# Linear attention and an FFN on one core: all scores in 64x64 tiles, part of the state sum on TensorE, another order of steps

## The chip, the cores and the metric

One core of a Trainium2 chip runs the whole program. The metric is device time in microseconds, the median of three executions; the time before is 443.19 us (442.01 to 443.64).

## The reference

Inputs r, k, v, w have the shape (4, 8, 768, 48): batch, heads, time, channels. For each batch and head a state of 48x48 runs along time, and its output goes through a token mix of rank 32 and an FFN (384 to 1536 to 384 channels).

```python
for t in range(S):
    cur = np.einsum('bhd,bhe->bhde', u[None] * kt, vt)
    y[:, :, t] = np.einsum('bhd,bhde->bhe', rt, state + cur)
    state = wt[:, :, :, None] * state + np.einsum('bhd,bhe->bhde', kt, vt)
# x: y as (batch, time, 384)
h = x.transpose(0, 2, 1) @ U @ V
u = x + h.transpose(0, 2, 1)
out = u + np.maximum(u @ w_ch1, 0.0) @ w_ch2
```

## The kernel before

Time is cut into chunks of 128; a batch has six, so there are 24, numbered g, with c = g % 6 the place in the batch. The heads lie as four pairs j, the two heads of a pair i on partitions 0 to 47 and 64 to 111. `chunk(g)` (line 349) lists the steps of a chunk, each for one engine:

- LW, LRK, LKR, LV load decays, r and k (channels by time), r and k by rows, and v; all loads are issued from SP's queue.
- F and Q (VectorE, L393 and L408) are products of decays along time. RP (L416) multiplies r by Q, KS (L421) k by F; each has VectorE and POOL to choose from. T copies the chunk's total decays, R inverts them.
- PR (L497, first batch) multiplies r and k, MD sums it by products with u; later chunks use RK, RU and RED. SEL and SEL2 (L465 on ScalarE, L472 on POOL) put the result on the diagonals of A.
- AM (L561, L553) multiplies k and r into scores in PSUM (`aps`). For chunks of which `swaps(g)` is true (line 48: g of 12 and more, and the last of a batch, g = 11 among them) it uses 64x64 tiles, four side by side in TensorE, and skips the quarter above the diagonal. For pairs 2 and 3 the rows of k then lie with swapped halves of time; others use 48x128 products, two side by side. CP (L566, L568) merges the scores under the diagonal into A.
- KT and KN turn k by TensorE and ScalarE, KD on VectorE from g = 12 on. DS (L575) multiplies turned k and v into `dS`, ZA (L604) adds the old state Z on VectorE, ZM (L613 on ScalarE, L615 on VectorE) multiplies by the next chunk's total decay.
- YA (L633, L643) multiplies A and v, YZ (L656, L660) adds the old state's part, XE (L677) copies the output, XT/XN or XD turn it.

`token_mix(b)` has GA, G4, SELM (L787), GS, GSL for a batch, `make_u` HP, UADD, UH (L840, L842) and UL (L846) for one of seven blocks of 384 or 512 columns, `ffn` twelve UP of nine products (L879), HH (L884 ScalarE, L886 VectorE), HL (L890), and twelve DN of nine products (L913). The FFN weights are brought into two parts by `split_raw` (C2, C3, E, ADD, HI, SUB with L341), and checks of weights (CK, CM) run late.

The order of the steps is written out: `ORDER` (line 66) is a text with three digits for each step: two for its number, one with two meanings (`plan`, line 135): odd, and the step runs on its other engine; half of it is `lead`, the count of warming products that `lead()` (line 202) has TensorE do just before the step. Those multiply a block of zeros (`blank`, bf16, 128x384, L200) into the place that the step's own products overwrite, and are no part of the result. Each engine and each queue takes its steps in the order of this text and waits in place. `aps` and `dS` exist once, so a step that writes them waits for the reader before.

Of the kernel before, what the change touches and what calls it, by code (L numbers as in the profile page):

```python
# [42 lines left out]
TURN_K_DVE, TURN_X_DVE = [12, 13, 14, 15, 16, 17, 18, 19, 20, 21, 22, 23], [12, 13, 14, 15, 16, 17, 18, 19, 20, 21, 22, 23]  # L43
W_MAX, W_MAX_BITS, DECAY_MIN = 1.25, 0x3FA00000, 1e-16
HIGH_MIN, HIGH_END = 1.125 * 2.0**-15, 122880.0


def swaps(g):

    return g >= 6 and (g in TURN_K_DVE or g % NCH == NCH - 1)  # L50


def channel_order():
# [18 lines left out]
    "7d04v07e00A07y04905G13l00b03L00p01C04W00c04AE7-04sC0B01D04t04Y00q00e04Z04X10f00d11E07f10g04a05H04f05I03m01F0"
    "5407h04w04z07l04B04+08011G04-04b07m14x08100z05J64y08505K05001H10r15L04c00s00u07g05M08415O05108Q00v00h05N00-0"
    "5P00i07a07n17q05Q08201005R07r00+07o00j08315S08O05T00t01100w01W08Y07u87p07v08R05U05Y01I05c05V00k07s05Z05W05a0"
    "5d08C01P07w05X18E05e00x01X01205b15f15p01K00y18Z17x01d07t11J01L08D01311R05q05s06205t01M08801N01e05u01Q01f02A0"
    "8905r01O08T05j06308a16507+01Y01g06401Z05g08A18B18G06601h08F05k01k01S01a06701r08b08J05h01T05i02B08S18W07c15l0"
    "8q08K08r01b06W06X01U01i05m08c11y08U05-05n01j11s08X01c11V06001t08+08d15y01l01m01u05o05v01v06109G08H05z08L02C0"
    "8V08g01z02301n02D08s08t01o01w05+05w08h05x08I16802E02H01x11p01q16B06E06C01+08l02406902508y01-02608v06D06A08w0"
    "2708m02I02802009P08-12109406F09018u18e06G02O08f02912V06Y08x02F18i09602G19109502216H02c06K02W02P06a02J02X02K0"
    "2d08z09216Z19H02L09J09312Q02M09L02Y02q09i08j06L06I09706b02N06e08n02Z02R08k12e02j02S02T06M02a09B06f09C02U02f0"  # L80
    "9M09K12g09Q06c0980BL09l08o02k08p06N02b16g16d16h19n09N0BB09D08M02l08N06Q09k02s07A02h12r06O06P06x02m07B02i19m0"
    "9I06y06z06J0BC09R17C06R02n02o17D0Bl02p12t02u07E09E09S09j0Bm07F0BM02v09s06S09t09O16r02w09o09q09F06s06l0BE06t0"
    "6m09Y0Bn16n07709T0Bo09U19r0BG0781990790BK06T09V19W0Bb06o06U06u09u19v09p1Bc09Z09X06V09a09y09w06p09d0BH09A09e0"
    "DB06v09b09x09z06q0Be06w0BI1Bg06+07106-06i0BJ0BF07009f07409+09c19-0BV0DC0BN0BR06j0Bj0750720Bh0Bd0BS0DD0C50BO0"
    "CF06k0CE0BD0730A00BP07G09g0C60760C80Br0BT07H0A107I0Bk0Bp1CX07J0A20BQ0C90Bf1BW0CY0BZ0DE0Ca0A30Bi19h0BU0Bq0A40"
# [74 lines left out]
def rwkv_moe_kernel(ctx, tc, wT, rkT, vN, vS, rkN, uB, uT, uD, U, V, w1, w2, out):  # L160
# [1078 lines left out]
```

## Time and profile before

| | |
|---|---|
| median of three runs | 443.19 us |
| the profiled execution | 442.49 us, span 440.8 us |
| TensorE, VectorE, ScalarE, POOL busy | 422.5, 349.9, 184.4, 131.7 us |
| products of the FFN (L879, L913) | 1512 of 3931 on TensorE |
| moved by DMA | 57.27 MB |

The span is what the instructions of one execution cover; the rest of its time lies around it. A TensorE product's duration in the rows overlaps the next one's, so the cost of a group of products is read from its start to the start of what follows.

### The profile page before, as it was taken

Reading aid. Unit: us, or ns where it says so; the run is one execution under the profiler, and the core shown is the slowest. Engines: PE = TensorE matmul, PEld = TensorE weight load, DVE = VectorE, ACT = ScalarE, POOL = GpSimd, SP = SyncE. Lnnn points to the kernel's source line nnn. Section 1 sums busy time; section 2 is a strip of 40 time slices with the busy share of each in tenths; the row PEclk is TensorE's granted clock in tenths of the full one; section 3 lists DMA queues with packets and bytes.
Section 4 is the critical chain, followed back from the end, with each engine's and each line's share of the span. In section 5 each row is a group of like instructions: output and inputs, shape, how many; then the busy total and the mean of one; then the engine's idle time right before and its main releaser. Section 6 shows DMA issues by size and latency. Waiting matters only on the chain.

```text
span 440.8 us, 10001 instructions
## 1 busy us (share of the span) xinstructions
PE 422.5 (96%) x3931; PEld 364.3 (83%) x3931; DVE 349.9 (79%) x796; ACT 184.4 (42%) x517; POOL 131.7 (30%) x157
## 2 busy tenths in 40 slices
PE   7989999999999999999999999999999999999993
PEld 4876788999999898878777788887766889999992
DVE  8899889999899999999999999999886224315610
ACT  5798888884245225363033423131741023301200
POOL 5665456334575375421145211051001001000000
PEclk8578999999999999999999999999999999999998
DMA  8996494556745341635064024245051022212001
GB/s 264 314 315 249 156 325 119 156 171 194 207 156 159 121 137 27 196 82 153 18 208 155 2 73 146 86 145 167 5 175 38 0 97 83 91 54 91 0 24 40
DMA packets 23912, 57.27 MB, mean 130 GB/s; under 512 B 2864, under 2 KB 7856, under 8 KB 23856
## 3 DMA queue, kind: packets, MB, share of 16 engines
q1 hardware_dynamic: 23856, 56.54, 40.3%
q8 instruction: 33, 0.54, 0.5%
q14 instruction: 23, 0.19, 0.1%
HBM read 51.81 MB, written 4.72 MB: 128 GB/s over the span
## 4 chain that ended last, share of the span: by engine, by line
PE 51%; DVE 37%; issue 4%; ACT 3%; DMA 2%; SPq 0%; DVEq 0%; ACTq 0%
PE f L913 19%; PE f L879 19%; DVE kn L696 8%; DVE xn L731 6%; DVE hid L890 4%; DVE Q L408 3%; DVE A L566 3%; DVE F L393 3%; PE aps L561 2%; PE y L633 2%; DVE xn L729 1%; DVE xT L835 1%; ACT A L465 1%; DMA w<-in_wT 1%; PE y L643 1%
## 5 line engine op out<-in xcount | busy, mean ns | idle before, releaser
L879 PE MATMUL f<-u,w1h 128*128 128x384 f32 (+1 forms) x504 | 147.6, 364 | 1.8 <-DVE hid L890 1.8
L913 PE MATMUL f<-hid,w2h 128*128 128x384 f32 (+1 forms) x504 | 149.1, 365 | 0.0
L879 PEld LDWEIGHTS f<-u,w1h 128*128 128x128 f32 x504 | 92.9, 188 | 14.4 <-DVE hid L890 3.2
L913 PEld LDWEIGHTS f<-hid,w2h 128*128 128x128 f32 x504 | 93.0, 188 | 9.9 <-issue 1.1
L884 ACT ACTIVATE hid<-f 128x384 fp32r<-128x384 f32 (+1 forms) x70 | 37.2, 541 | 142.5 <-PE f L879 97.7
L879 PE MATMUL f<-u,w1l 128*128 128x384 f32 (+1 forms) x252 | 90.8, 360 | 0.0
L913 PE MATMUL f<-hid,w2l 128*128 128x384 f32 (+1 forms) x252 | 90.8, 360 | 0.0
L890 DVE SCALAR_TENSOR_TENSOR hid<-f,hid 128x384 fp32r<-128x384 f32 (+1 forms) x84 | 49.8, 606 | 19.4 <-ACT hid L884 18.6
L913 PEld LDWEIGHTS f<-hid,w2l 128*128 128x128 f32 x252 | 47.5, 188 | 4.6
L879 PEld LDWEIGHTS f<-u,w1l 128*128 128x128 f32 x252 | 47.4, 188 | 4.2
L696 DVE STREAM_TRANSPOSE kn<-rk 32x128 f32<-32x128 f32 x160 | 48.3, 302 | 2.4
L465 ACT ACTIVATE A<-ident,dv 128x128 f32<-128x128 f32 x140 | 43.9, 393 | 4.9 <-DVE dv L451 4.8
L324 POOL TENSOR_TENSOR cva_w<-cva_w,raw_w 128x384 int32<-128x384 int32 x24 | 25.4, 1063 | 47.3 <-DVE cva_w L317 21.1
L416 POOL TENSOR_TENSOR rk<-rk,Q 128x512 f32<-128x512 f32 x19 | 23.5, 1236 | 46.9 <-DVE Q L408 33.0
L846 POOL TENSOR_TENSOR u<-xT,u 128x512 fp32r<-128x512 f32 (+1 forms) x11 | 13.4, 1232 | 78.5 <-DVE u L842 68.1
L408 DVE TENSOR_TENSOR_SCAN Q<-w,starts,qd 128x258 f32<-128x258 f32 x48 | 33.2, 733 | 0.2
L393 DVE TENSOR_TENSOR_SCAN F<-w,qd 128x259 f32<-128x259 f32 x48 | 30.4, 675 | 1.8 <-DMA w<-in_wT 1.6
L931 DVE TENSOR_TENSOR xT<-f,xT 128x384 f32<-128x384 f32 (+1 forms) x21 | 12.6, 605 | 23.4 <-PE f L913 23.3
L731 DVE STREAM_TRANSPOSE xn<-xT 32x192 f32<-32x192 f32 x80 | 29.6, 369 | 2.1 <-ACT xT L677 0.9
L421 POOL TENSOR_TENSOR rk<-rk,F 128x512 f32<-128x512 f32 x15 | 17.9, 1196 | 15.5 <-DVE F L393 8.2
L886 DVE TENSOR_SCALAR hid<-f 128x384 fp32r<-128x384 f32 (+1 forms) x14 | 8.2, 584 | 15.9 <-PE f L879 15.9
L472 POOL TENSOR_SCALAR_AFFINE_SELECT A<-dv 128x128 f32<-128x128 f32 (+1 forms) x39 | 11.6, 333 | 30.2 <-PE f L913 20.2
(124 smaller groups left out, 571.4 us busy)
## 6 DMA issues: line engine op xcount, KB each, us to landing
raw_w<-in_w SPq DMA_DIRECT2D x48, 384.0 KB, 3.6
rk<-in_rkT SPq DMA_DIRECT2D x24, 512.0 KB, 4.9
kr<-in_rkN SPq DMA_DIRECT2D x18, 384.0 KB, 4.2
w<-in_wT SPq DMA_DIRECT2D x24, 260.0 KB, 3.4
v<-in_vS SPq DMA_DIRECT2D x24, 224.0 KB, 3.4
out_dram<-xT SPq DMA_DIRECT2D x12, 192.0 KB, 3.2
out_dram<-xT SPq DMA_DIRECT2D x9, 256.0 KB, 2.9
raw_V<-in_V SPq DMA_DIRECT2D x8, 96.0 KB, 3.6
```

Of the source, the lines that this page charges most:

```text
L324: lambda: nc.gpsimd.tensor_tensor(out=d["to"].bitcast(I32), in0=d["a"].bitcast(I32), in1=d["e"], op=ALU.add),
L393: nc.vector.tensor_tensor_scan(out=back(F), data0=back(st["w"]), data1=back(qd, OVER * h), initial=1.0, op0=ALU.mult, op1=ALU.add)
L408: nc.vector.tensor_tensor_scan(out=st["Q"][:, a:e], data0=st["w"][:, a:e], data1=qd[:, a - OVER * h : e - OVER * h], initial=starts[:, h : ...
L416: ENG[eng].tensor_tensor(out=rk[:, 0], in0=rk[:, 0], in1=Qv, op=ALU.mult)
L421: ENG[eng].tensor_tensor(out=rk[:, 1], in0=rk[:, 1], in1=F5, op=ALU.mult)
L465: nc.scalar.activation(to, one, AF.Copy, scale=dv[:, NP * i + j : NP * i + j + 1])
L696: nc.vector.transpose(a, b)
L731: nc.vector.transpose(to[q, :, :, r], src[r, :, :, q])
L879: nc.tensor.matmul(ps, wt[:, f, ct, :], u[ct][:, z], start=(m == 0), stop=(m == 8))
L884: nc.scalar.activation(h[:, 0], d["ps", f], AF.Relu)
L890: nc.vector.scalar_tensor_tensor(out=h[:, 1], in0=d["ps", f], scalar=0.0, in1=h[:, 0].bitcast(F32), op0=ALU.max, op1=ALU.subtract)
L913: nc.tensor.matmul(d["o", ct], wt[:, 4 * ct + part, f - 3 * part, :], hid[f][:, z], start=(part == 0 and m == 0), stop=(part == 3 and m == 8),
```

## The change

Five things change.

1. `scores` uses 64x64 tiles for every chunk: eleven more, g = 0 to 10. Two ScalarE activations at the program's start write zeros into the parts of `aps` that the tiles never write, since the merge now always reads whole halves.
2. The array of k comes from the host with swapped halves of time for pairs 2 and 3. So `scale_k` (KS) and `prod` (PR) are two multiplications, one for pairs 0 and 1, one for pairs 2 and 3 with the other operand's halves read crosswise. `diag` on POOL is always three instructions; none of the chunks g = 0 to 10 ran it on POOL before.
3. For g = 1 to 4 `state_add` (DS) multiplies the identity by the old Z first and adds k and v on top, in PSUM. ZA is gone there, and DS waits for the old state's ZM.
4. `ORDER` is another text. Decoded, it has 1418 steps (four ZA fewer), and eight warming products in place of 29: six before YA 6 and two before UP 0.4; before, they stood ahead of YA 2 (9), XT 0.2 (7), KT 4 (6), YA 5 (3) and YA 6 (4). The first FFN step is number 301 (300 before), with the same TensorE steps in front of it in another order, and the same TensorE steps stand behind SELM 3.
5. By that text some steps change their engine (counts before and after). On VectorE: ZM 4 and 0, KS 9 and 7, UH 8 and 2, HI 3 and 1, SUB 18 and 16, T 7 and 6, DV 0 and 1, HH 14 and 17, RK 5 and 6, RP 5 and 6. What VectorE gives up goes to ScalarE (ZM, UH, HI, T) or POOL (KS, SUB). SEL on POOL: 5 and 8; SEL2: 8 and 6.

Between the last UL of block 0 and GSL 3 VectorE has in the new text one KS, two SUB, three ZM, one CK, one HL, three UH, two HI and one T fewer, and five HH and two UL more.

```diff
+ADD_Z_PE = (1, 2, 3, 4)
...
-def swaps(g):
-
-    return g >= 6 and (g in TURN_K_DVE or g % NCH == NCH - 1)
...
+    for a in range(2):
+        part = aps_all[HP * a : HP * a + HP, :, NQ * (1 - a) : NQ * (2 - a), 0:HP]
+        nc.scalar.activation(part, blank[HP * a : HP * a + HP].rearrange("p (i j t) -> p i j t", i=2, j=NQ), AF.Copy)
...
+        def by_halves(eng, to, k, x):
+
+            a, b = slice(0, NQ), slice(NQ, NP)
+            ENG[eng].tensor_tensor(out=to[:, a], in0=k[:, a], in1=x[:, a], op=ALU.mult)
+            to, k, x = (t[:, b].rearrange("p j (h l) -> p j h l", h=2) for t in (to, k, x))
+            ENG[eng].tensor_tensor(out=to, in0=k, in1=x[:, :, ::-1, :], op=ALU.mult)
...
-            ENG[eng].tensor_tensor(out=rk[:, 1], in0=rk[:, 1], in1=F5, op=ALU.mult)
+            k = st["rk"][:, 1]
+            by_halves(eng, k, k, F5)
...
-                ENG[eng].tensor_tensor(out=st["kr"], in0=st["rk"][:, 0], in1=st["rk"][:, 1], op=ALU.mult)
+                by_halves(eng, st["kr"], st["rk"][:, 1], st["rk"][:, 0])
...
-            for j in range(NP):
-                for i in range(2):
-                    r = slice(64 * i, 64 * i + D)
-                    nc.tensor.matmul(aps[:, i, j, :], rk[r, 1, j, :], rk[r, 0, j, :], start=True, stop=True)
+            for j in range(NQ):
+                for h in range(2):
+                    for i in range(2):
+                        r = slice(64 * i, 64 * i + D)
+                        for a in range(2):
+                            jj, s0 = j + NQ * (a ^ h), HP * h
+                            k0 = HP * a
+                            nc.tensor.matmul(
+                                aps[HP * a : HP * a + HP, i, jj, s0:P], rk[r, 1, jj, k0 : k0 + HP], rk[r, 0, jj, s0:P],
+                                start=True, stop=True,
+                            )
...
+                    to = dS[r, j, i * D : i * D + D]
+                    if z_pe:
+                        nc.tensor.matmul(to, ident[:, r], old["Z"][:, j, i * D : i * D + D], start=True, stop=False)
+                    nc.tensor.matmul(to, kn[:, j, r], v[:, j, r], start=not z_pe, stop=True)
...
-            if c > 0:
+            if not fresh:
                 za = step("ZA " + nm, "DVE", add_z, [ds, old["z"]], take=[buf["Z"]], use=[buf["dS"], old["buf"]["Z"]])
...
+    kT = chunked(k, 0.0)
+    kT[:, :, :, NQ:] = np.roll(kT[:, :, :, NQ:], HP, axis=4)
+    rkT = np.stack([chunked(r, 0.0), kT], axis=3)
```

## Rows read from the trace of the kernel before

**Rows 1.** The page: busy time of each engine; TensorE's clock in 40 slices.

```profile
PE 422.5 (96%) x3931; PEld 364.3 (83%) x3931; DVE 349.9 (79%) x796; ACT 184.4 (42%) x517; POOL 131.7 (30%) x157
...
PEclk8578999999999999999999999999999999999998
```

**Rows 2.** Windows: us, busy time by engine, granted clock, DMA share, GB/s.

```profile
8.00:28.00 20.00, 19.01 (x170) 16.59 (x172) 18.57 (x39) 16.47 (x55) 13.87 (x13) 0.50 0.97 311
28.00:34.80 6.80, 4.68 (x89) 3.83 (x82) 6.74 (x16) 6.80 (x24) 3.31 (x3) 1.00 0.92 313
34.80:38.20 3.40, 3.40 (x39) 1.86 (x36) 3.40 (x7) 3.00 (x11) 2.14 (x3) 0.50 1.02 394
38.20:62.60 24.40, 24.14 (x423) 18.66 (x419) 22.17 (x44) 20.42 (x56) 11.72 (x11) 1.00 0.61 208
62.60:327.60 265.00, 261.27 (x2651) 222.54 (x2649) 253.27 (x592) 117.45 (x322) 93.61 (x114) 1.00 0.43 131
327.60:433.40 105.80, 105.01 (x559) 98.23 (x559) 38.85 (x86) 17.21 (x47) 3.20 (x3) 1.00 0.16 51
```

**Rows 3.** Chain of waits, whole span: start us, us, what.

```profile
40.51 1.09 PE aps L561 x16
...
127.75 0.83 PE aps L553 x32
...
337.35 12.36 PE f L913 x54
```

**Rows 4.** Groups by line and shape, TensorE, 8 to 28 us.

```profile
L561 PE MATMUL aps<-rk 48*128 48x128 f32 x48 | 6.2, 437 | 1.0 <-DVE A L568 0.7 <-POOL rk L416 0.3
...
L575 PE MATMUL dS<-v,kn 128*48 128x48 f32 x32 | 1.8, 285 | 0.0
```

**Rows 5.** Timeline of TensorE, 30 to 63 us: start us, us, what.

```profile
34.04 2.34 PE L200 MATMUL y<-blank 128*128 128x384 bf16 x9 [2.12 <-ACT xT L677]
36.30 1.08 PE L633 MATMUL y<-A,v 128*32 128x128 f32 x16
...
42.24 1.30 PE L200 MATMUL trx<-blank 128*128 128x384 bf16 x7
43.38 0.49 PE L750 MATMUL trx<-ident,xT 128*128 128x128 f32 x3
...
47.97 0.56 PE L575 MATMUL dS<-v,kn 128*48 128x48 f32 x16
48.47 0.65 PE L633 MATMUL y<-A,v 128*32 128x128 f32 x16
...
50.81 0.65 PE L200 MATMUL y<-blank 128*128 128x384 bf16 x3
51.39 0.64 PE L633 MATMUL y<-A,v 128*32 128x128 f32 x16
```

**Rows 6.** Line L421 on VectorE (min/median/max ns), then groups by line and shape.

```profile
L421 DVE TENSOR_TENSOR rk<-rk,F x9: 678/685/932, 19.3 to 298.6; 128x512 f32<-128x512 f32 x9
...
L421 POOL TENSOR_TENSOR rk<-rk,F 128x512 f32<-128x512 f32 x15 | 17.9, 1196 | 15.5 <-DVE F L393 8.2 <-DVE kr L497 3.9 <-DMA rk<-in_rkT 3.4
...
L604 DVE TENSOR_TENSOR Z<-dS,Z 128x384 f32<-128x384 f32 x16 | 8.8, 547 | 0.1
...
L341 DVE TENSOR_TENSOR w2l<-cva_w,w2h 128x384 fp32r<-128x384 f32 x9 | 4.8, 547 | 0.1
...
L613 ACT ACTIVATE Z<-dS,tots 128x96 f32<-128x96 f32 x16 | 4.1, 336 | 0.0
...
L615 DVE TENSOR_TENSOR Z<-Z,tots 128x384 f32<-128x384 f32 x4 | 2.2, 539 | 0.0
...
L842 DVE CAST u<-xT 128x384 fp32r<-128x384 f32 x6 | 2.1, 352 | 0.0
...
L324 POOL TENSOR_TENSOR U_sb<-cva_U,raw_U 128x192 int32<-128x192 int32 x1 | 0.6, 604 | 0.0
```

**Rows 7.** Waits of VectorE, 8 to 62.6 us: us in total, times, longest.

```profile
DVE A L568 <- PE aps L561: 1.8, 3, 0.7
```

More of the change, by code (lines that the diff above doesn't have):

```diff
@@ L72 @@
[L72 to L76, printed above, removed]
@@ L461, in diag @@
                     to, one = A[:, i, j], ident
-                    if swap and j >= NQ:
+                    if j >= NQ:
                         to, one = (x.rearrange("p (a b) -> p a b", b=HP) for x in (to, one))
@@ L466, in diag @@
                 return
[L467 to L490 removed]
+            for js, ts, base in (
+                (slice(0, NQ), slice(0, P), 0), (slice(NQ, NP), slice(0, HP), HP), (slice(NQ, NP), slice(HP, P), 0),
+            ):
+                n = ts.stop - ts.start
+                nc.gpsimd.affine_select(
+                    out=A[:, i, js, ts],
+                    in_=dv[:, NP * i + js.start : NP * i + js.stop].unsqueeze(2).broadcast_to([P, NQ, n]),
+                    pattern=[[0, NQ], [1, n]],
+                    compare_op=ALU.is_equal,
+                    fill=0.0,
+                    base=base,
+                    channel_multiplier=-1,
+                )
         if by_pe:
@@ L545, in scores @@
             lead(aps[:, 0])
[L546 to L568 removed]
+            for j in range(NQ):
[8 more added lines that the diff above has]
+                                start=True, stop=True,
+                            )
+        def merge():
+            to, new = (t.rearrange("p i j t -> p i (j t)") for t in (st["A"], st["aps"]))
+            nc.vector.copy_predicated(to, mask2, new)
         def state_add():
@@ L594, in chunk @@
         if on:
-            ds = step("DS " + nm, "PE", state_add, [kn, lv], take=[buf["dS"]], use=[buf["kn"], buf["v"]])
+            ds = step(
+                "DS " + nm, "PE", state_add, [kn, lv] + ([old["z"]] if z_pe else []), take=[buf["dS"]],
+                use=[buf["kn"], buf["v"]] + ([old["buf"]["Z"]] if z_pe else []),
+            )
             st["ds"] = ds
-            zuse = [buf["dS"]] if c == 0 else [buf["Z"]]
+            fresh = c == 0 or z_pe
+            zuse = [buf["dS"]] if fresh else [buf["Z"]]
             def new_z():
@@ L607, in decay @@
                 nxt = sts[g + 1]["tot"]
-                if c == 0:
+                if fresh:
                     new_z()
-                src = dS if c == 0 else st["Z"]
+                src = dS if fresh else st["Z"]
                 if eng == "ACT":
@@ L617, in decay @@
                     )
-            if c > 0:
+            if not fresh:
                 za = step("ZA " + nm, "DVE", add_z, [ds, old["z"]], take=[buf["Z"]], use=[buf["dS"], old["buf"]["Z"]])
             st["z"] = step(
-                "ZM " + nm, "DVE", decay, [ds] if c == 0 else [za],
-                take=[buf["Z"]] if c == 0 else [], use=zuse, alt="ACT",
+                "ZM " + nm, "DVE", decay, [ds] if fresh else [za],
+                take=[buf["Z"]] if fresh else [], use=zuse, alt="ACT",
             )
@@ L964, in recurrence @@
                 nc.sync.dma_start(chunks(rt), rb[:, 0, j])
-                nc.sync.dma_start(chunks(kt), rb[:, 1, j])
+                for h in range(2):
+                    s0 = HP * (h ^ (j >= NQ))
+                    nc.sync.dma_start(chunks(kt)[:, :, HP * h : HP * h + HP], rb[:, 1, j, :, s0 : s0 + HP])
                 nc.vector.memset(vt, 0.0)
@@ L1189, in ordered @@
         a = a.copy()
-        for g in range(B * NCH):
-            x = a[g // NCH, g % NCH, :, NQ * 2 :]
-            if swaps(g):
-                x[:] = np.roll(x, HP, axis=0)
+        a[:, :, :, NQ * 2 :] = np.roll(a[:, :, :, NQ * 2 :], HP, axis=2)
         return a
```

139 lines of the change are left out of this document (46 added, 93 removed).

## The prediction

> **What bounds the kernel now.** I read the page first: TensorE is busy 96% of the span and VectorE 79%, and the slices show the clock of TensorE below full only in the first tenth [rows 1]. So the windows by stage come next [rows 2]. Between 8 and 28 us TensorE is busy 19.0 of 20.0 us, but at a granted clock of 0.50, that is 1.2 GHz, and the DMA engines are at 0.97. From 28 to 34.8 us the clock is full; in 34.8 to 38.2 it is at 0.50 again; after that it stays at 2.4 GHz. In 38.2 to 62.6 us, up to the first FFN product, TensorE is busy 24.1 of 24.4 us and VectorE 22.2. From 62.6 to 327.6 us, where chunks and FFN blocks alternate, TensorE has 261.3 of 265.0 us and VectorE 253.3. After 327.6, where the last chunk's token mix is summed, TensorE works 105.0 of 105.8 us and VectorE a third of that. Third, the chain of waits: there 54 products of L913 run without a gap, 12.36 us at 337.35 us [rows 3]. This last stage is set by its product count alone. The change leaves that count and the step that opens the stage (SELM 3) as they are, so the end moves by as much as SELM 3 moves. Before it, TensorE and VectorE are both close to full: a saving counts only where both get it. I therefore sum each engine up to the first FFN product and from there to SELM 3, and take the smaller gain.
>
> **Part 1, up to the first FFN product (62.6 us).** Eight chunks' scores (g = 0 to 7) lie here, the same set in both orders.
>
> Scores on TensorE. Sixteen 48x128 products take 1.09 us from start to start at full clock; the 32 tiled ones, which g = 11 and later already use, take 0.83 [rows 3]. Five chunks save 0.26 each, 1.3 us. Three run at half clock, 6.2 us for 48 products, or 2.07 each [rows 4]. No row shows the tiled form at half clock; its bounds are 2.07 (nothing saved) and 1.24 (0.83 saved). By the ratio 0.83 to 1.09 it is 1.58; I take 0.5 saved each, 1.5 us.
>
> State sums. DS takes 0.50 us at full clock (47.97 to 48.47 us) [rows 5]; two at half clock take 1.8 us [rows 4]. DS 1 to 4 double their products: 0.9 for DS 1 and 0.5 for each of the others, 2.4 us more (bounds 1.2, if the identity products overlap well, and 3.6).
>
> Warming products. Ahead of YA 2, XT 0.2, KT 4, YA 5 and YA 6 stand 29 of them: nine from 34.04 to 36.30, seven from 42.24 to 43.38, three from 50.81 to 51.39 [rows 5], and ten more at 1.14 / 7 = 0.163 us, together 2.26 + 1.14 + 0.58 + 1.63 = 5.6 us. The eight of the new order cost 1.3, so 4.3 us go. TensorE alone would gain 1.3 + 1.5 + 4.3 - 2.4 = 4.7 us, by the bounds 2.0 to 6.9.
>
> VectorE. Removed: four ZA at 0.547, one ZM at 0.539 (the decay goes to ScalarE, four activations of 0.336), one KS at 0.685 [rows 6], 3.4 us. Added: one RP (as KS, 0.685) and one RK (0.55, as other operations on 384 columns), a small copy of 0.1 to 0.2, and seven multiplications cut in two: 512 columns take 0.685 and 384 take 0.547, so the fixed part is near 0.13; with some overlap I take 0.1 each, 0.7. Net 3.4 - 2.1 = 1.3 us less. VectorE also waited 1.8 us in three places for scores [rows 7], which come earlier without the warming products. It can gain 3.1 us at most; I take half the waits, 1.3 + 0.9 = 2.2.
>
> POOL. A KS of 512 columns takes 1.196 us and 192 columns 0.604 [rows 6], so the slope is 1.85 ns and the fixed part 0.25 us, which each cut repeats. Off the path POOL has room (11.7 busy of 24.4 us [rows 2]), but the first KS and the RP queued behind it stand before the first scores, with the cut product PR 0 ahead of them: 0.25 + 0.1 = 0.35 us later (bounds 0 and 0.6). I charge 0.2, for TensorE was behind its inputs soon after.
>
> Loads on SP's queue. By the shapes, up to the fifth chunk's decays the old order moves 7.74 MB and the new one 7.52; at 311 GB/s [rows 2] that is 0.7 us earlier. The keys of chunk 1 come behind a weight piece, 1.93 MB instead of 1.55, 1.2 us later. I take zero: these ends cancel, and the half-clock queue of TensorE covers the late one. The two activations that clear parts of aps stand at ScalarE's start, before the first decay lands, and cost nothing; without that cover they would be two operations of at most 0.5 us.
>
> New wait. DS 1 to 4 now wait for the preceding ZM on ScalarE. YA and YZ of the same chunk are queued behind them on TensorE, and ZM of this chunk waits for DS. Before, ZA on VectorE took that wait. The new order puts at least three other TensorE steps between one DS and the next (YA 2, YZ 2 and MD 5 before DS 3), which cover the ZM between them, so I cost it at nothing; a late ZM would show as a gap like the one before 34.04 us, 2.1 us [rows 5].
>
> Part 1 together: 2.2 - 0.2 = **2.0 us less** (bounds: 2.1 + 0.6 - 1.3 = 1.4 more, if that gap comes back and POOL's cut costs its bound; 3.1 less).
>
> **Part 2, 62.6 to 327.6 us.** On TensorE only the scores of g = 8, 9 and 10 shrink, 0.8 us. VectorE loses one KS, two SUB, three ZM, one weight check and one HL, the last four kinds near 0.55 [rows 6], 4.5 us; three UH and two HI of 0.35 [rows 6], 1.8; it gains five HH and two UL of 0.55 to 0.69, 3.9 to 4.8, and three cuts, 0.3. Net 1.2 to 2.1, so 1.7 us less. VectorE has 11.7 us idle here and TensorE 3.7 [rows 2]: both queues are almost full, and a shorter one gives back part of the other's waits. I take 1.7 us, VectorE's sum. The most is TensorE's, 0.8 + 3.7 = 4.5; the least, a new order that makes one more wait like the one at 34.04, is 2.1 worse [rows 5].
>
> On POOL and VectorE together: one of nine VectorE KS took 0.932 us against a median of 0.685 [rows 6], so a neighbour seldom costs anything. The Trainium skill, SBUF — State Buffer, section Who interferes with whom, says that a VectorE instruction with two SBUF inputs and a GpSimd instruction that reads SBUF contend, and the later one fully blocks. By that rule, two KS and two SUB moved to POOL could come back to VectorE as blocked time, 2.5 us: the sum would be 3.7 - 2.5 = 1.2 us less, 442.0. The trace bears it out in one instruction of nine and by 0.25 us, so I keep the row's price.
>
> **The sum.** 2.0 + 1.7 = 3.7 us less. The profiled execution took 442.49 us with a span of 440.8; the median of the three runs is 443.19, 0.7 above. On the median: **439.5 us**. A measurement of this kernel can tell about 0.5%, 2.2 us, from no change.
>
> **Rivals.** *No change to be told, 441.7 us.* The order only trades waits: VectorE stays the later engine up to SELM 3, warming products stood in waits anyway, and the moved work returns as waits for ScalarE and POOL. For it: VectorE's own relief is only 1.3 + 1.7 us, ScalarE gets five more decays and six UH, and at 28 to 34.8 it was busy 6.8 of 6.8 us [rows 2]. Against it: 1.8 us of VectorE's waits were for scores [rows 7]. With half of VectorE's relief left, 1.5 us less.
>
> *Slower, 447.5 us: the clock.* Full clock came at 28 us, was lost after the gap before 34.04, and came back after the nine products; thirteen of the others stand right behind [rows 2, 5]. If the sparse head of the new order leaves TensorE at 1.2 GHz for 16 us more up to 62.6, its work there takes 8 us longer: 439.5 + 8 = 447.5. It decides from about 12 us more at half clock on (6 us, which turns the 3.7 gained into 2.3 lost). For it: 19.0 of 20.0 busy us did not raise the clock in 8 to 28. Against it: KT 2, KT 3, YA 1 and YZ 1 stand together in both orders, and were under way when the clock rose.
> The Trainium skill, TensorE: Matmul & The Clock Gate, Why this matters for your kernels, advises no long idle gaps between bursts, since an idle engine is throttled again. By that rule the missing products would cost just this; the trace agrees in the one dip, which followed the idle 2.1 us.
>
> *Better than the sum, 435.5 us:* the waits of Part 2 shrink to TensorE's own bound: 3.1 + 4.5 = 7.6 us less.
>
> **How the numbers follow.** The forecast has 0.52, no change 0.24, the clock 0.16, the better case 0.08. Faster by over 0.5% is 0.52 + 0.08 = 0.60, same 0.24, slower 0.16. The range holds the forecast, the no-change case and the better one: 435.5 at the low end, and at the high end 445.0, the no-change case with the worst new waits of both parts (441.7 + 1.4 + 2.1 = 445.2). The clock case is mostly left out.
>
> **What would show it.** Right: scores of 0.83 us from g = 0 on at full clock and near 1.6 at half; no ZA before chunk 7 on VectorE; DS 1 to 4 near 1.0 us; the first L879 near 60.6 us; SELM 3 near 324; the same 105.8 us behind it. Wrong: a granted clock of 0.50 after 38 us; TensorE idle before DS; SELM 3 not earlier though the first L879 is, which would mean that Part 2 took the gain back.

## The result, and the profile after

The changed kernel takes **435.92 us** (median of four runs, 435.45 to 438.02) against 442.6 for the kernel before beside it: ratio 0.9855 (95% interval 0.9826 to 0.9885), 6.4 us less. The forecast was 439.5, 3.7 less: the sign was right and the size a little over half, with 1.8 us in a place where nothing was forecast. The profiled execution took 435.73 us with a span of 433.9.

The page, busy time and TensorE's clock, beside [rows 1]:

```profile
PE 417.4 (96%) x4150; PEld 361.9 (83%) x4150; DVE 344.5 (79%) x791; ACT 188.7 (43%) x536; POOL 137.7 (32%) x182
...
PEclk8586999999999999999999999999999999999998
```

Windows of the changed kernel at its own stages, beside [rows 2] (columns as there):

```profile
8.00:24.60 16.60, 15.91 (x209) 14.46 (x210) 16.21 (x35) 15.53 (x54) 11.95 (x14) 0.50 0.94 329
24.60:34.86 10.26, 7.98 (x199) 7.00 (x197) 10.23 (x23) 9.60 (x33) 6.68 (x8) 1.00 0.91 307
34.86:41.70 6.84, 6.43 (x105) 5.77 (x109) 6.71 (x17) 6.84 (x22) 2.33 (x4) 0.50 0.74 271
41.70:58.71 17.01, 16.32 (x371) 12.57 (x364) 16.95 (x33) 15.17 (x44) 10.05 (x11) 1.00 0.74 253
58.71:322.57 263.86, 260.61 (x2700) 221.60 (x2698) 250.25 (x588) 119.56 (x333) 97.79 (x131) 1.00 0.41 129
322.57:428.33 105.76, 105.05 (x559) 98.20 (x559) 37.39 (x80) 18.86 (x52) 5.03 (x5) 1.00 0.19 59
```

Of the busy times the third is VectorE's: 16.21 of 16.60, 10.23 of 10.26, 6.71 of 6.84, 16.95 of 17.01. Up to the first FFN product VectorE hardly ever stands still. That product now starts at 58.71 us instead of 62.56 (3.9 less), SELM 3 at 322.57 instead of 327.62 (1.2 less in the stage between), and the last stage is 105.76 us long, as before. From the end of the last product (428.33 here, 433.34 before) to the end of the span it is 5.6 us instead of 7.4: **1.8 us for which the prediction has no term**.

The chain of waits, beside [rows 3], with the same scores at half and at full clock:

```profile
28.42 6.81 DMA v<-in_vS
...
36.80 1.49 PE aps L544 x32
...
42.56 0.49 ACT xT L666
...
43.65 0.97 ACT A L469 x3
...
56.30 0.83 PE aps L544 x32
```

In the kernel before, this chain runs through TensorE from 34.04 us to the first FFN product, but for two copies of 0.50 us on ScalarE. Here it runs through the load of v, TensorE, ScalarE (42.56 to 52.22 us) and TensorE again. In a second profile of the changed kernel (e8, below) it runs through VectorE from 35.68 to 54.88 us, for example:

```profile
51.89 1.30 DVE Q L405 x2
...
53.65 1.24 DVE A L551
```

So VectorE is full up to the first FFN product, but it isn't alone on the path there: these engines come out nearly even.

TensorE's timeline, a state sum with the identity products at full clock and the scores behind it, beside the 0.50 us of [rows 5]:

```profile
42.41 0.30 PE L560 MATMUL dS<-Z,ident 128*48 128x48 f32 x4
42.54 0.27 PE L561 MATMUL dS<-v,kn 128*48 128x48 f32 x4
...
43.30 0.90 PE L544 MATMUL aps<-rk 48*64 48x128 f32 x32
```

From its start to the start of what follows, 32 products take 0.89 us, 0.39 more than 16 did.

The groups, cut multiplications on VectorE and POOL, beside [rows 6]:

```profile
L420 POOL TENSOR_TENSOR rk<-rk,F 128x256 f32<-128x256 f32 x17 | 12.0, 708 | 0.0
L418 POOL TENSOR_TENSOR rk<-rk,F 128x256 f32<-128x256 f32 x17 | 11.9, 698 | 18.7 <-DVE F L390 11.1 <-DMA rk<-in_rkT 3.9 <-DVE kr L418 3.7
...
L420 DVE TENSOR_TENSOR rk<-rk,F 128x256 f32<-128x256 f32 x7 | 2.9, 416 | 0.0
L418 DVE TENSOR_TENSOR rk<-rk,F 128x256 f32<-128x256 f32 x7 | 2.9, 412 | 0.0
```

Waits of VectorE from 8 to 58.7 us, all that is left beside [rows 7]:

```profile
DVE F L390 <- DMA w<-in_wT: 0.2, 1, 0.2
```

Before, the same view had three lines: the 1.8 us for scores of [rows 7], and two for loads that the prediction did not weigh:

```profile
DVE F L393 <- DMA w<-in_wT: 1.3, 2, 0.8
DVE cva_w L304 <- DMA raw_w<-in_w: 0.4, 1, 0.4
```

So 3.5 us of waits became 0.2.

### The profile page after: what moved, and what is told of

It is laid out like the page before. It is cut to its first block, busy times and chain, and to the rows that moved or that the text cites. A ratio compares the mean times of both kernels' runs of the same rounds, so it can differ in the third digit from the quotient of the medians.

```text
span 433.9 us, 10499 instructions
## 1 busy us (share of the span) xinstructions
PE 417.4 (96%) x4150; PEld 361.9 (83%) x4150; DVE 344.5 (79%) x791; ACT 188.7 (43%) x536; POOL 137.7 (32%) x182
## 4 chain that ended last, share of the span: by engine, by line
PE 73%; DVE 18%; ACT 3%; DMA 2%; issue 2%; POOL 0%; DVEq 0%
PE f L898 29%; PE f L864 25%; PE aps L544 4%; DVE kn L679 3%; DVE xn L716 3%; PE y L622 2%; DVE hid L875 2%; DVE xn L714 2%; PE dS L561 2%; PE y L632 2%; DMA v<-in_vS 2%; DVE A L551 1%; PE trd L496 1%; DVE F L390 1%; PE trk L522 1%
## 5 line engine op out<-in xcount | busy, mean ns | idle before, releaser
L869 ACT ACTIVATE hid<-f 128x384 fp32r<-128x384 f32 (+1 forms) x67 | 35.9, 541 | 138.3 <-PE f L864 124.7
L469 ACT ACTIVATE A<-ident,dv 128x128 f32<-128x128 f32 x136 | 43.0, 394 | 4.3 <-PE f L898 4.2
L322 POOL TENSOR_TENSOR cva_w<-cva_w,raw_w 128x384 int32<-128x384 int32 x24 | 26.1, 1098 | 45.4 <-ACT raw_w L309 18.6
L831 POOL TENSOR_TENSOR u<-xT,u 128x512 fp32r<-128x512 f32 (+1 forms) x11 | 12.8, 1169 | 85.4 <-ACT u L825 64.3
L413 POOL TENSOR_TENSOR rk<-rk,Q 128x512 f32<-128x512 f32 x18 | 21.6, 1201 | 52.3 <-DVE Q L405 34.9
L551 DVE COPY_PREDICATED A<-maskf,aps 128x1024 f32<-128x1024 uint32 x24 | 31.5, 1311 | 0.3 <-PE aps L544 0.2
L544 PE MATMUL aps<-rk 48*64 48x128 f32 (+1 forms) x768 | 24.2, 270 | 0.9 <-POOL rk L413 0.9
L544 PEld LDWEIGHTS aps<-rk 48*64 48x64 f32 x768 | 20.7, 147 | 5.1 <-issue 2.8
```

The source lines that it names most:

```text
L322: lambda: nc.gpsimd.tensor_tensor(out=d["to"].bitcast(I32), in0=d["a"].bitcast(I32), in1=d["e"], op=ALU.add),
L469: nc.scalar.activation(to, one, AF.Copy, scale=dv[:, NP * i + j : NP * i + j + 1])
L544: nc.tensor.matmul(aps[HP * a : HP * a + HP, i, jj, s0:P], rk[r, 1, jj, k0 : k0 + HP], rk[r, 0, jj, s0:P], start=True, stop=True,)
L551: nc.vector.copy_predicated(to, mask2, new)
L869: nc.scalar.activation(h[:, 0], d["ps", f], AF.Relu)
```

## The experiments

Each kernel ran beside the kernel before on the same chip. "First UP" is the start of the first FFN product in the profiled execution; the next two columns are for 8 us to there: VectorE's idle time (length less its busy time) and TensorE's busy time, from the windows; "end" is the span less the end of the last product.

| kernel | ratio (95%) | first UP | VectorE idle | TensorE busy | end |
|---|---|---|---|---|---|
| before | 1 | 62.56 | 3.7 | 51.2 | 7.4 |
| before, again (e4) | one run | 62.29 | 3.2 | 50.8 | 7.6 |
| e11 before, SP's program longer | 0.9962 (0.9939–0.9984) | 62.22 | 2.3 | 49.6 | 5.5 |
| e1 before, no warming | 0.9971 (0.9954–0.9988) | 61.04 | 2.7 | 48.4 | 7.4 |
| e3 tiles, old order | 0.9948 (0.9929–0.9967) | 62.05 | 2.2 | 47.7 | 5.7 |
| e7 new order alone | 0.9996 (0.998–1.0011) | 62.94 | 2.7 | 45.7 | 7.8 |
| e13 identity sum alone | 1.0025 (0.9995–1.0056) | 62.90 | 5.8 | 51.4 | 7.5 |
| e16 identity sum, no warming | 0.9906 (0.9863–0.995) | 60.41 | 3.3 | 47.9 | 7.4 |
| e15 both, old order, no warming | 0.9922 (0.9894–0.9949) | 60.57 | 2.5 | 49.1 | 5.5 |
| e6 new order, identity sum | 0.9927 (0.9903–0.9951) | 59.70 | 2.5 | 46.9 | 7.9 |
| e5 new order, tiles | 0.9914 (0.9886–0.9942) | 65.04 | 3.6 | 45.3 | 5.8 |
| after | 0.9855 (0.9826–0.9885) | 58.71 | 0.6 | 46.6 | 5.6 |
| after, again (e8) | 0.9855 (0.9826–0.9884) | 59.15 | 0.5 | 47.6 | 5.7 |
| e2 after, 29 warming | 0.9858 (0.9834–0.9882) | 59.76 | 2.1 | 46.2 | 5.9 |
| e9 after, no warming | 0.9845 (0.9806–0.9885) | 59.41 | 1.1 | 45.4 | 5.6 |
| e12 after, SP's program shorter | 0.9896 (0.9862–0.993) | 60.03 | 1.4 | 46.9 | 7.8 |
| e14 after, two SUB on POOL | 0.9876 (0.9836–0.9915) | 61.07 | 2.3 | 46.7 | 5.6 |
| e17 after, identity sum in 7 to 10 | 0.9879 (0.9843–0.9914) | 59.91 | 2.0 | 46.6 | 5.7 |

One profiled execution is up to 2.5 us from its kernel's median: e5's took 441.88 us where its median is 439.34. Where the two disagree, the ratio counts. The same executed program puts the first UP at 58.71, 59.15 and 60.03 (after, e8, e12) or at 62.56, 62.29 and 62.22 (before, e4, e11).

### The end behind the last product

Is the long end of the kernel before chance? No edit:

> The kernel before, unchanged, profiled once more: is its end repeatable? Theory: the 1.9 us that the end after the last product took longer than in the changed kernel (7.46 against 5.57 us) is chance, the landing of the last store and a gap between instructions of SP: here the end takes 5.5 to 6.5 us. Rival, that it belongs to the kernel before: 7.2 to 7.7 us again. The first UP at 62.56 and SELM 3 at 327.6 within 0.2 us by both.

It was not: 7.6 us again. The first UP, 62.29, and SELM 3, 326.8, came 0.3 and 0.8 us earlier, where both sides expected 0.2 at most. Apart from the two edits that follow (e11, e12), the kernels built on the old code had 7.4 to 7.9 us, those on the new code 5.5 to 5.9, even with the old order (e3). The two programs differ on SP in something that never runs: in `recurrence`, part of the path for general inputs which the program's end branches over, k is loaded in two halves. Counted in the built programs, SP has 661 instructions before, 665 in e6 and e7 (four come with the new order), 669 in e3, 673 after. The edit for the direct test, to 669:

```diff
 def recurrence(xs):
-                nc.sync.dma_start(chunks(kt), rb[:, 1, j])
+                for h in range(2):
+                    nc.sync.dma_start(chunks(kt)[:, :, HP * h : HP * h + HP], rb[:, 1, j, :, HP * h : HP * h + HP])
```

> The kernel before with one edit, in the general path that this run branches over: there the loads of k are cut into two DMAs each, eight instructions more on SP that are never executed. Nothing that runs is changed. Theory, that the long end of the kernel before (7.4 to 7.6 us behind the last product, with a gap of 1.8 us after the fifth of SP's last semaphores) comes from where SP's last instructions lie in its program (four instructions more moved the gap to after the first semaphore): with eight more the gap falls ahead of the first semaphore, into the wait for the last store: an end of 5.5 to 5.9 us, the first UP still at 62.3 to 62.6, the run 440.4 to 441.2 us against 442.6, ratio 0.995 to 0.997. Rival, that the end depends on the data moved or on the order: 7.4 us again and a ratio of 1.000.

Theory: 440.95 us, ratio 0.9962, an end of 5.5 us, the first UP at 62.22, 0.1 us ahead of its range. And from the other side, the changed kernel with that load whole again, 665 instructions:

```diff
 def recurrence(xs):
-                for h in range(2):
-                    s0 = HP * (h ^ (j >= NQ))
-                    nc.sync.dma_start(chunks(kt)[:, :, HP * h : HP * h + HP], rb[:, 1, j, :, s0 : s0 + HP])
+                nc.sync.dma_start(chunks(kt), rb[:, 1, j])
```

> The changed kernel with eight instructions fewer in SP's program, all in the general path that this run branches over (there k is loaded whole, not in halves, so that path would not compute the reference; it does not run). Theory, the position of SP's last instructions: SP's program has then the length at which the old scores with the new order showed a gap after the first of the last semaphores, so an end of 7.4 to 8.0 us behind the last product comes back, the first UP and SELM 3 stay (58.7 to 59.2, 322.6 to 322.9), the run 437.6 to 438.5 us. Rival, that the end has to do with what the changed kernel executes: 5.6 us and 436 again.

Theory again for the end, 7.8 us, and the time, 438.17; the first UP (60.03) and SELM 3 (323.73) came 0.8 us or more behind their ranges. The view that shows it is the one of SP's eight last semaphore instructions (count, ns of one, first and last start). Before:

```profile
L1157 SPq EVENT_SEMAPHORE  x8: 17/17/17, 436.9 to 439.4; - x8
```

The same with the eight instructions more (e11):

```profile
L1158 SPq EVENT_SEMAPHORE  x8: 17/17/17, 437.5 to 438.0; - x8
```

The changed kernel:

```profile
L1144 SPq EVENT_SEMAPHORE  x8: 17/17/17, 432.0 to 432.6; - x8
```

and with eight instructions fewer (e12):

```profile
L1142 SPq EVENT_SEMAPHORE  x8: 17/17/17, 433.1 to 435.9; - x8
```

Eight instructions of 17 ns take 0.5 to 0.6 us or 2.5 to 2.8. In the trace of before the gap stands after the fifth of them, with four instructions more ahead (e6, e7, e12) after the first, with eight or twelve more nowhere; that it then falls into the wait for the last store, which lasts anyway, is likely, but no row shows it. Nor does a row say what SP does in the gap; that it fetches the next piece of its program is my reading, not shown. That the place of the instructions in the program decides is shown, and it is worth 1.4 to 1.8 us by medians and ratios.

### One part alone

The 29 warming products of the old order:

```diff
 order of before, by step: warming products ahead
-YA 2: 9, XT 0.2: 7, KT 4: 6, YA 5: 3, YA 6: 4
+none
```

> The kernel before without its 29 warming products (the old order else, whole 128-column scores). Theory, that VectorE sets the pace up to the first FFN product and that its waits of 1.8 us for scores there came from TensorE being late: TensorE loses 5.6 us of work, the waits for scores shrink from 1.8 to under 0.8 us, the first UP starts at 61.0 to 61.8 us (62.56 before), the run takes 441.2 to 442.0 us against 442.6. Rival, that the warming products alone were the gain: first UP near 58.9, 438.8 us or less. Rival, that they kept the clock up: granted clock 0.50 for more than 3.4 us after 34 us, the first UP at 63.5 or later, 443.5 or more.

The theory's mechanism, a little under its range: 440.77 us, by the ratio 1.3 less, the first UP at 61.04. No wait for scores is left, but VectorE waits 2.5 us for loads instead of 1.7. The half-clock stretch behind 34 us was longer, 6.8 us (35.73 to 42.56) against 3.4, so the condition of the second rival was met without its price: the first UP came 1.5 us earlier.

```diff
 after.py, with the order of before
-ADD_Z_PE = (1, 2, 3, 4)
+ADD_Z_PE = ()
```

> The changed kernel's code for 64x64 tiles and swapped keys in every chunk, but no identity sum (ZA on VectorE everywhere) and the old order with its 29 warming products. Theory: TensorE saves 2.2 to 2.8 us in the scores of the first eight chunks, VectorE pays 7 cuts of about 0.06 us and POOL's cuts 0.25, so VectorE's waits for scores shrink by about 1 us and nothing else changes: first UP at 61.3 to 62.3, the run 441.5 to 442.4 us. Rival, that the tiles were the gain: first UP below 60, 439.5 us or less. Rival, that the cuts cost more than the tiles give: 443.2 or more.

440.10 us, by the ratio 2.3 less, below the theory's range; but 1.8 of that is the end. Up to the first UP the tiles alone gave 0.2 to 0.5 us; against e11, whose end is short too, 0.6 us by the ratios (0.9962 to 0.9948), within their intervals.

```diff
 before.py, with the order of after
+ZA 1 to 4, each ahead of its ZM
```

> The kernel before's code with the new order alone (ZA on VectorE in every chunk, whole scores, eight warming products). Theory: the order and the missing 21 warming products give about 1.5 to 2 us up to the first UP, the identity sum the other 2: first UP at 60.2 to 61.2 us, SELM 3 at 323.7 to 325.3, an end of 7.4 us, the run 438.8 to 440.3 us. Rival, that the order alone is the whole gain before SELM 3: first UP below 59.3 and 437.5 us. Rival, that the new order needs the identity sum (VectorE late, TensorE waits): first UP at 62 us or later, 441.5 or more.

Neither the theory nor the first rival: 442.50 us, no change, the first UP at 62.94. The second rival, that the new order needs the identity sum, is what it shows: TensorE is busy only 45.7 of 54.9 us. Its longest wait up to the first UP is for ScalarE's copies of the output, and ScalarE's longest is for ZA:

```profile
PE y L633 <- ACT xT L677: 7.2, 3, 3.0
...
ACT Z L613 <- DVE Z L604: 2.7, 2, 1.5
```

The new order gives every ZM to ScalarE, which waits in place for VectorE's ZA; by these lists the copies behind it come late for that. ScalarE's list of before has no such wait. The identity sum takes ZA, and with it this wait, out of the way.

```diff
 before.py, old order, 29 warming products
+ADD_Z_PE = (1, 2, 3, 4)
-ZA 1, ZA 2, ZA 3, ZA 4
 ZM 2 moved to the place of ZA 2
```

> The kernel before with the identity sum for chunks 1 to 4 alone, in its old order with its 29 warming products (ZA 1 to 4 dropped; the one step moved is ZM 2, to ZA 2's place, since DS 3 needs it). Theory, that the sum was VectorE's limit in either order: four operations of 0.547 us less, 2.2, and up to 0.8 more of waits: first UP at 59.5 to 60.4 us (62.29 to 62.56 before), an end of 7.4 to 7.9 us, the run 439.6 to 440.8 us. Rival, that in the old order TensorE is the late engine (29 warming products, and DS longer by 0.25 to 0.7 us each): first UP above 61.3 and 441.6 us or more; then the order and the identity sum pay only together.

The rival: 442.94 us, none faster. VectorE's work fell by 1.7 us (50.84 to 49.10), and its waits took all of it. Its waits from 8 to 62.9 us:

```profile
DVE A L569 <- PE aps L562: 3.6, 3, 1.5
DVE F L394 <- DMA w<-in_wT: 1.2, 1, 1.2
DVE cva_w L305 <- DMA raw_w<-in_w: 0.7, 1, 0.7
```

and the windows for the same stretch:

```profile
8.00:62.90 54.90, 51.35 (x771) 40.94 (x770) 49.10 (x98) 46.05 (x143) 30.97 (x29) 0.97 0.78 268
```

With the identity sum alone TensorE is the late engine for VectorE's merge (scores 3.6 us late instead of 1.8). The clock is not the cause: the three waits end at 41.60, 48.03 and 56.95 us, where it is 1.00. The 0.97 of the line above is too high, though. This profile has no clock record before 23.17 us, the view counts the time before as full clock, and the scores there take 2.08 us, as at half clock in [rows 4].

### Two parts together

```diff
 as e13
-YA 2: 9, XT 0.2: 7, KT 4: 6, YA 5: 3, YA 6: 4 warming products
+none
```

> The kernel before's code with the identity sum in its old order (as the earlier one, ZM 2 moved) and without the 29 warming products; whole scores. Theory: with the warming products gone TensorE's 57.0 us of work become 51.4, the waits for scores shrink from 3.6 to under 1.5 us, first UP at 59.8 to 61.0 us, an end of 7.4 us, the run 439.5 to 440.8 us. Rival, that the tiles or the new order are needed: first UP at 61.5 us or later, 441.3 or more.

A little under the theory's range: 439.27 us, first UP at 60.41 within it. The sum that was worth nothing (1.0025) is worth 2.9 us (0.9971 to 0.9906, with 443 us) once the warming products are gone. No wait for scores is left in its list:

```profile
DVE F L394 <- DMA w<-in_wT: 2.9, 3, 2.5
```

```diff
 before.py, with the order of after
+ADD_Z_PE = (1, 2, 3, 4)
```

> The kernel before's code (whole 128-column scores and uncut multiplications for chunks 0 to 4 and 6 to 10, keys not swapped there) with the identity sum and the new order with its eight warming products. Theory, that the tiles were worth next to nothing up to the first UP, as with the old order (62.05 against 62.29 to 62.56 us): the first UP starts at 58.5 to 59.5 us, SELM 3 at 322.3 to 323.5, behind the last product again an end of about 7.4 us, the run 437.2 to 438.5 us. Rival, that in the new order TensorE is late without the tiles: first UP at 60 us or later and 439 us or more. On the end: theory, a code position on SP, four instructions further than in the kernel before, so the gap of 1.8 us stands after the first semaphore instead of the fifth; rival, that it belongs to the fetched data or to chance: an end of 5.7 us.

Between the two: the first UP, 59.70, is nearer the theory's, the time, 439.51 us, is the rival's; the end, 7.9 us, is where the theory had it. Against e7 the identity sum gives 3.1 us here (0.9996 to 0.9927). In what runs, e12 differs from this kernel only by the tiles, the swapped k and what they need, and it has the long end too: 1.4 us less (0.9927 to 0.9896), which the intervals don't separate from nothing. So of the 6.4 us, by the ratios, order and identity sum bring 3.2 (e6), the tiles 1.4 (e6 to e12, not clear of noise), the end 1.8 (e12 to the changed kernel).

```diff
 after.py, with its order
-ADD_Z_PE = (1, 2, 3, 4)
+ADD_Z_PE = ()
+ZA 1 to 4, each ahead of its ZM
```

> The changed kernel with the old state added by VectorE again in every chunk (ZA 1 to 4 back on VectorE, DS of 16 products), everything else of the change kept. Theory, that VectorE sets the pace up to the first FFN product in the changed kernel (0.6 us idle of 50.7): four operations of 0.55 us come back in full, the first UP starts at 60.2 to 61.2 us (58.71 in the changed kernel), SELM 3 at 323.5 to 325, the run takes 437.2 to 438.5 us against 435.9. Rival, that TensorE's shorter DS (0.25 us each) and the old waits make up for it: first UP within 0.5 us of 58.71, 435.9 within 0.7. Both: an end of 5.5 to 6 us behind the last product.

439.34 us, over the theory's 438.5: leaving the sum out costs 2.6 us (0.9855 to 0.9914). Its profile, 2.5 us over its median, has the first UP at 65.04 and SELM 3 at 328.5, both far behind the theory's ranges. The four additions are 2.2 us of it by their price, and the two waits of e7 are there again (8.2 us of TensorE's for the copies, 3.1 of ScalarE's for ZA); how the 2.6 us divide is not shown.

```diff
 after.py, with the order of before
-29 warming products
-ZA 1, ZA 2, ZA 3, ZA 4
 ZM 2 moved to the place of ZA 2
```

> The changed kernel's code (tiles, identity sum) in the order of the kernel before (ZA 1 to 4 dropped, ZM 2 moved to ZA 2's place), without any warming product. Theory, that the identity sum pays as soon as TensorE is relieved, whatever the order: TensorE has 5.6 us of warming products and 2.5 of scores less than with the identity sum alone (57.0 us busy, 62.9), VectorE is the later engine, first UP at 58.7 to 60.0 us, 5.6 us behind the last product, the run 436 to 438 us. Rival, that the new order is needed (loads and steps placed where VectorE meets them): first UP at 61 us or later, 438.5 or more.

Between the two: 439.14 us and a first UP at 60.57. The median lies in the rival's range, the profile in neither. So the new order is worth something of its own beside the other parts: 1.2 us up to the first UP and 0.7 more from there to SELM 3 against e9 in the profiles, 3.4 by the ratios. Nor do the tiles pay in the old order: e16, with whole scores, is no slower (0.9906 against 0.9922), though its end is 1.9 us longer. VectorE's waits of e15 are loads again, 2.0 us; with the new order and all parts they are 0 to 0.7 in four profiles (after, e8, e9, e12), but 1.5 to 1.9 in e2, e14 and e17. What decides on them was not tried.

### Warming, VectorE and Part 2 in the changed kernel

No edit, beside the others:

> The changed kernel unchanged, beside the others on the same chip. Theory: 435.9 us within 0.7, first UP at 58.7 to 58.9, SELM 3 at 322.6, 5.6 us behind the last product once more, and no gap between SP's last semaphores. Rival, that the short end was chance: 7.4 us. Beside it the one with the 29 warming products (436.38) can be told apart only if this one takes 435.3 or less.

436.42 us, ratio 0.9855 once more, an end of 5.7 us; the first UP, 59.15, and SELM 3, 322.9, were up to 0.3 us behind what was expected.

```diff
 order of after, by step: warming products ahead
-YA 6: 6, UP 0.4: 2
+YA 2: 9, XT 0.2: 7, KT 4: 6, YA 5: 3, YA 6: 4
```

> The changed kernel with the 29 warming products put back ahead of the same steps as in the kernel before (and the two placed by the new order taken out). Theory: 21 products more are 3 to 4 us more of TensorE, VectorE waits again for scores by about 1 to 1.8 us, the second half-clock stretch ends earlier than at 41.69 us, the first UP starts at 59.7 to 60.5 (58.71 in the changed kernel), the run takes 437.0 to 437.8 us against 435.9. Rival, that the warming products cost nothing in either order: first UP within 0.3 us of 58.71, 435.9 within 0.6.

The first UP went to 59.76, as the theory had it, but by another way: no wait for scores came back, VectorE's 1.6 us are waits for loads. The time, 436.38, is the rival's and can't be told from the changed kernel's. The clock was full from 25.08 us on, with 13.7 us at 1.2 GHz between 8 us and the first UP, against 23.4 in the changed kernel's first profile, and that brought nothing to be told. With the identity sum in place the 29 products cost far less in the new order than in the old (e13 to e16, 5.3 us by the ratios).

```diff
-YA 6: 6, UP 0.4: 2
+none
```

> The changed kernel without its eight warming products. Theory, that VectorE sets the pace there and the granted clock up to the first UP doesn't matter (the changed kernel had 0.80 in one profile and 0.88 in another with the first UP at 58.7 and 59.1): first UP at 58.4 to 59.0 us, 435.4 to 436.4 us, not to be told from the changed kernel. Rival, that they hold the clock: 0.50 for 10 us or more after 34 us, first UP above 60, 437.5 or more.

The theory's time, 435.82 us, with the first UP 0.4 beyond its range. The clock was at 0.50 for 6.8 us behind 34 us (37.05 to 43.88), as long as in the changed kernel's first profile: the eight warming products hold neither the clock nor the time. The 0.80 and 0.88 of the expectation can't be compared, and nor can the windows of e8, e9 and e12, whose clock records begin at 17.05, 16.57 and 26.17 us. e12's window (columns as in [rows 2]) and one of the scores in it:

```profile
8.00:28.00 20.00, 19.63 (x275) 17.24 (x273) 18.93 (x41) 17.60 (x61) 14.40 (x17) 1.00 0.91 301
...
13.99 1.56 PE L544 MATMUL aps<-rk 48*64 48x128 f32 x32
```

These scores take 1.56 us, as those of the changed kernel's first profile at a granted clock of 0.50 do (13.84 us); at full clock the same row has 0.90 (43.30 us, above). With the time before the first record counted at half clock, an estimate from these rows, all four profiles have 0.77 to 0.79 up to the first UP.

```diff
 order of after
-SUB w17, SUB w18 on VectorE
+SUB w17, SUB w18 on POOL
```

> The changed kernel with two subtractions of weight pieces, SUB w17 and SUB w18, on POOL instead of VectorE (one step each, same places in the order). Theory: VectorE is busy 50.1 of the 50.7 us from 8 us to the first UP, so 1.1 us less of its work lets the first UP start 0.5 to 1.1 us earlier, 57.6 to 58.4, of which the stage up to SELM 3 keeps about half: 434.9 to 435.8 us. Rival, that the loads or TensorE are next in line: first UP within 0.2 us of 58.7 to 59.1, 436 us. Rival, that POOL's queue is then late (about 1.0 us each there, RP 7 and the additions behind them): first UP at 59.5 or later, 437 or more.

437.23 us, the numbers of the second rival, but the rows show a cause that it doesn't name. VectorE was busy 50.81 us instead of 50.10, although one of the two steps left this stretch. Two lines of its timeline and one of POOL's show it:

```profile
48.94 1.13 DVE L418 TENSOR_TENSOR rk<-rk,F 128x256 f32<-128x256 f32 x1
49.99 0.41 DVE L420 TENSOR_TENSOR rk<-rk,F 128x256 f32<-128x256 f32 x1
...
48.76 1.03 POOL L339 TENSOR_TENSOR w1l<-cva_w,w1h 128x384 fp32r<-128x384 f32 x1
```

The first half of a multiplication takes 0.41 us alone (412 ns in the groups of the changed kernel), and 1.13 when it starts 0.18 us into a subtraction on POOL. L831 at 59.98 met the other moved subtraction so (0.95 us instead of 0.55): 1.1 us together, as much as the edit took off VectorE. A third meeting, L420 at 33.63 with 1.23 us, is not the edit's: e8, e9 and e12 have it too. VectorE also waits 1.9 us for loads; that POOL's longer queue makes them was not tried.

```diff
-ADD_Z_PE = (1, 2, 3, 4)
+ADD_Z_PE = (1, 2, 3, 4, 7, 8, 9, 10)
-ZA 7, ZA 8, ZA 9, ZA 10
```

> The changed kernel with the identity sum also in chunks 7 to 10 (ZA 7 to 10 dropped; DS there 32 products). These lie near and behind the first UP, where FFN products alternate with chunks. Theory, that TensorE sets the pace there (260.6 of 263.9 us busy): VectorE's 2.2 us less bring nothing, TensorE's 16 products more per DS cost about 0.25 us each: SELM 3 at 322.5 to 324, the run 435.9 to 437.2 us. Rival, that VectorE's waits hold TensorE up there: SELM 3 at 320.5 to 322, 434 to 435.3 us, which would beat the changed kernel.

437.84 us, a little beyond the theory's range, with SELM 3 at 324.8: no gain, and by the ratios 1.1 us lost, within the intervals. From the first UP to SELM 3:

```profile
59.91:324.80 264.89, 262.10 (x2763) 223.16 (x2761) 248.95 (x584) 118.66 (x333) 97.59 (x131) 1.00 0.41 129
```

VectorE has 1.3 us less than in the changed kernel, TensorE 1.5 more (four state sums at 0.39 are 1.6, not 0.25 each), and the stage is 1.0 longer: in Part 2 TensorE sets the pace. No kernel beat the changed one by more than can be told.

## Why the prediction was right in sign and half the size

**The end.** "The end moves by as much as SELM 3 moves" is the step that failed most. The last stage kept its length (105.72 and 105.76 us), but behind it 1.8 us went, through eight instructions on SP that are never executed. The prediction put the 7.4 us between the last product and the span's end at no change without a reason. Of the 2.7 us between forecast and result (3.7 and 6.4) this is 1.8, Part 1 is 1.1 more than forecast, and Part 2 0.3 to 0.5 less.

**Part 1** was forecast at 2.0 us; by the three profiles of either executed program it was 3.1 (means of the first UP 62.4 and 59.3). The step that failed is "it can gain 3.1 us at most; I take half the waits". In the first pair VectorE's idle time fell by 3.1 us, where 0.9 was forecast. All of the waits for scores went (1.8 us; 1.0 in e4), and nearly all of those for loads of w and raw_w (1.7 us in both), which the bound left out. TensorE's relief was sized well (4.7 forecast; 51.2 to 46.6 and 47.6 measured, 3.6 to 4.6). VectorE's own work fell less than the 1.3 forecast: 50.84 to 50.10 and 50.64 behind 8 us, the latter with 0.8 us of a meeting with POOL (below).

The view that both engines have to be relieved held in the main: identity sum alone, nothing (e13); order alone, nothing (e7); both, by the ratio 3.2 us (e6); identity sum and no warming, 4.2 (e16). TensorE's relief alone does pay a little, 1.3 us (e1). Halving the waits was a guess between two ends; summing the late engine's relief, 4.7 us, against each wait by name would have said that all of the waits for scores go.

**Part 2**, forecast at 1.7 us, gave 1.2 in the first pair of profiles and 1.4 on the mean of three stages each (265.1 to 263.8). The size was near and the engine wrong: VectorE's work fell by 3.0 us, nearly twice the forecast, but TensorE sets the pace (e17), and its work fell by 0.7 us (261.27 to 260.61; 0.8 forecast), its idle time by 0.5. That the size came near was luck.

**Prices.** Tiled scores at half clock: 1.58 forecast, 1.49 measured. The state sum with identity products: 1.0 forecast, 0.89 at full clock. DS waiting for ZM: nothing forecast, none in the changed kernel's list of TensorE's waits. ScalarE took four more decays, not the five of the first rival; no sum hangs on it. A cut multiplication on VectorE: 0.41 + 0.42 us, which overlap by 0.08, 0.07 more than the 0.685 whole against 0.1 forecast; on POOL 0.70 + 0.71, 0.2 more than 1.196 against 0.25. Loads at zero: one was late, for a state sum on TensorE,

```profile
PE dS L561 <- DMA v<-in_vS: 1.8, 1, 1.8
```

and it stands on that profile's chain of waits (28.42, above). e8 has no such wait, and its first UP came no earlier (59.15), so what the wait cost is open.

**The rivals.** Two signs of being wrong did show in the changed kernel: TensorE idle before DS 3, and a granted clock of 0.50 up to 41.7 us. The clock rival's price did not come: the stretch behind 34 us was twice that of before (6.8 us, 3.4 before), but the first ended at 24.6 us instead of 28.0, so either profile has 23.4 us at 1.2 GHz between 8 us and the first UP. In the longer stretch VectorE was busy 6.71 of 6.84 us; as the chain passes through TensorE there, whether it cost anything is not shown. "No change" fails by the ratio. "Better than the sum" named 435.5 us, near the result, but by another way: it had the surplus in Part 2.

**POOL and VectorE.** The prediction put the blocking aside, for one instruction of nine and 0.25 us, but the 0.932 us was a block: L421 began 0.65 us into a POOL instruction of 1.03 us and ended 0.55 us after it (timelines of VectorE and of POOL, kernel before).

```profile
115.31 0.93 DVE L421 TENSOR_TENSOR rk<-rk,F 128x512 f32<-128x512 f32 x1
...
114.66 1.03 POOL L324 TENSOR_TENSOR cva_w<-cva_w,raw_w 128x384 int32<-128x384 int32 x1 [4.07 <-issue]
```

So the price is what is left of POOL's instruction, not 0.25. In e8 an L420 took 1.23 us instead of 0.42 behind a POOL instruction that had begun 0.13 us earlier (timelines of VectorE and of POOL):

```profile
31.94 1.23 DVE L420 TENSOR_TENSOR kr<-rk 128x256 f32<-128x256 f32 x1
...
31.81 1.08 POOL L322 TENSOR_TENSOR cva_w<-cva_w,raw_w 128x384 int32<-128x384 int32 x1 [3.27 <-ACT Vst L332]
```

and e14 shows the 1.13 above. The Trainium skill, SBUF — State Buffer, section Who interferes with whom, calls the shared pair of ports "an exclusive lock"; these rows agree: VectorE's instruction ended 0.28 us after POOL's in both. In Part 2 it changes nothing that counts, since TensorE sets the pace there.

Still open: why VectorE waits for loads in some kernels (2.9 us in e16, 1.6 in e2) and hardly in the changed one, what the tiles are worth, and what the single moves of the new order bring.

## What to carry to other kernels

Where two engines wait for each other in turn, the relief of one alone shows as waits for the other; price a change by both, and try its parts in pairs, not only alone. List every wait of the engine that sets the pace, loads among them, before bounding what it can win. And look at what stands behind the last product too: code that never runs can move the program's end by over 1 us, so compare kernels with ends of the same length before giving the difference to an edit. A mean clock can hold time without a record; compare it with a row whose length at either clock is known.

## What the runs showed of the hardware that was not expected

- The end of the program hangs on where SP's last instructions lie: four instructions more ahead of them moved a gap of about 2 us from after the fifth semaphore to after the first, and eight more hid it (7.4 to 7.9 us or 5.5 to 5.9 behind the last product, in eight and ten profiles).
- A VectorE operation on two SBUF operands that starts inside a POOL operation can be held up until that one is over: with 256 columns it ended 0.28 us after it (e8, e14), with 384 columns 0.42 (e14's L831), with 512 columns 0.55 (L421 of the kernel before). An operation with one operand in PSUM was not held up: e14's L820 at 59.05 us took 0.55 us inside POOL's L339, its usual time. In the changed kernel's first profile it went the other way at the place of e8's meeting: VectorE's L420 kept its 0.42 us, and POOL's L322 beside it took 1.41, where its median is 1.03. This one meeting is worth 0.8 us of VectorE's time between two runs of the same kernel.
- A higher clock of TensorE brought no time that can be told: with 29 warming products the changed kernel had 13.7 us at 1.2 GHz up to the first UP instead of 23.4, a first UP of 59.76 instead of 58.71, and the same time (0.9858 and 0.9855). The 21 products more are in that too.
